# Decode attention on one core: masks from the identity, and cache rows dealt to the partitions in another order

## The chip, the cores and the metric

The kernel runs on one core of a Trainium2 chip. The metric is the device time of one execution in microseconds (us), as the median of several runs; lower is better. Beside it there is one profiled execution, whose trace gives every number below that has no other source.

## What is computed

Two decode-attention blocks, A and B, each for 4 batches, one query token, 32 query heads, 8 key/value heads and a head size of 128. Each projects `x` with `wq`, attends over its cache and projects with `wo`. A reads all 8192 cached tokens, B only the last 2048. Cut to what matters:

```
q = (x @ wq) in heads                         # 4 query heads share one kv head
s = einsum("bhqd,bhkd->bhqk", q, k) * 128**-0.5
o = einsum("bhqk,bhkd->bhqd", softmax(s), v)
out_A = o @ wo                                # k, v: all 8192 tokens
out_B = the same with k, v = the last 2048    # concatenated behind A
```

Softmax and the weighted sum run over all tokens of a head, so the order in which the tokens of one head are held does not matter, as long as keys and values are held alike and each stays with its head.

## The kernel before

**Units.** The work is cut into 20 units: first 4 of B (one batch each, all 8 kv heads), then 16 of A (one batch and one pair of kv heads each: `gp` is the pair). Every unit holds 4 MB of keys and 4 MB of values, as 128 partitions of 128 token slots of 128 bf16 numbers, in `K_sb` and `V_sb`, which have two slots each. For an A unit the source is one stretch of 128 rows of 32 KB (a row is 128 tokens); rows 0 to 63 belong to the first head of the pair, rows 64 to 127 to the second. Before the change partition p holds row p, so partitions 0 to 63 hold the first head. A B unit is loaded differently: K in two transfers of four heads, V in four of two heads, and there the source's outer dimension counts the row in the head and the next one the head, so that heads alternate along the partitions (L739).

**One unit.** TensorE transposes K through PSUM banks (`pe_T`, L271), ScalarE and VectorE copy the result to `KT_sb` (L299), and TensorE multiplies with the query (`pe_S`, L312). VectorE takes the maximum over the tokens of each partition (`dve_max`, L413), and `dve_addmask` (L430) adds `MASK[P]`, which is 0 where partition and column belong to the same head and -1e30 elsewhere; GpSimd then takes the maximum over the partitions (`pool_ar1`, L437), and `dve_submask` (L444) subtracts the mask again, so that the exponentials of a wrong head come out as zero. P @ V of the unit before follows (`pe_PV`, L327), and once for each head group the output projection.

**Order.** Each engine has a list of operations in `plan`, filled by `op`; `emit` and `emit_loop` write it out with its semaphore waits. TensorE, VectorE and ScalarE run in a loop of two units. All large loads are issued by SP's queue in the order in which `kv_load` (L722) is called: the two `wq` (into the V slots), K of unit 0, then for each u K of unit u and V of unit u-1, with a 1 MB piece of `wo` before some. A load waits for its slot to come free (the `w` lists in `kv_load`). The last unit's V comes in five pieces, and the last `wo` piece in eight.

**Setup.** GpSimd writes `MK` (`pool_mask0`, L522) and `MASK[0]` (`pool_mask1`, L530) by eight small memsets, then constants and zeros (`pool_setup0`, L537), then `ident` and `identf` (`pool_setup1`, L549) and `permE` (L557). It then issues two DMAs (L569 to L576) that copy the two halves of `MK` to the even and odd partitions of `MASK[1]`, in which heads alternate. `dve_msk` (L564) makes `MSK` and `SEL` from `ident`. TensorE waits for it before its loop (L594).

Of the kernel before, what the change touches and what calls it, by code (L numbers as in the profile page):

```python
# [7 lines left out]
F32 = mybir.dt.float32  # L8
I32 = mybir.dt.int32
ACTF = mybir.ActivationFunctionType  # L10
AX = mybir.AxisListType
# [3 lines left out]
def bass_concat_heads__gqa_block_cached__sliding_block_cached__decode_kernel(  # L15
# [16 lines left out]
    _, HKV, SK, DH = A_k_cache.shape  # L32
    HQ = A_wq.shape[1] // DH
    REP = HQ // HKV
# [3 lines left out]
    NT = SK // 64  # L38
    NSEG = 4
    TS = NT // NSEG  # L40
    C = 2 * REP
# [4 lines left out]
    BIG = 1.0e30  # L46
# [8 lines left out]
    NTH = NT // 2  # L55
# [4 lines left out]
    WQ = [A_wq, B_wq]  # L60
# [12 lines left out]
    with ExitStack() as es:  # L73
        block = es.enter_context(nc.Block())

        def sb(name, shape, dt):
            return es.enter_context(nc.sbuf_tensor(name, shape, dt))
# [4 lines left out]
        def sm(name):  # L82
# [7 lines left out]
        ident = sb("ident", [128, 128], BF16)  # L90
# [3 lines left out]
        RQ = [sb("RQ%d" % P, [128, Bn, NSEG, 2, 2 * C], BF16) for P in range(2)]  # L94
        RQc = sb("RQc", [128, 2, NSEG, 2, 2 * C], BF16)
        permE = sb("permE", [128, 2, 2, 64], BF16)
        MK = sb("MK", [128, NSEG * C], F32)
        MASK = [sb("MASKA", [128, C], F32), sb("MASKB", [128, NSEG * C], F32)]
        M1 = sb("M1", [128, NSEG * C], F32)
        M1m = sb("M1m", [128, NSEG * C], F32)  # L100
# [14 lines left out]
        ORx = sb("ORx", [C * Bn, C, C, 128 // C], BF16)  # L115
        MSK = sb("MSK", [C * Bn, C], BF16)
        SEL = sb("SEL", [C * Bn, Bn], BF16)
        OL = sb("OL", [128, C, Bn], BF16)
        oacc = sb("oacc", [Bn, D], F32)
        osb = sb("osb", [Bn, 2, D], BF16)  # L120
# [5 lines left out]

        names = ["k0", "k1", "kh", "v0", "v1", "vl0", "vl1", "vl2", "vl3", "vl4", "wl0", "wl1", "wl2", "wl3", "wl4", "wl5", "wl6", "wl7", "x0", "x1", "w0", "w1", "wo",
                 "out0", "out1", "out2", "Tq", "Td", "Ta", "S", "PV", "Ed", "Ea", "Eq", "vs", "sub", "exp", "otr", "otp",
                 "ocp", "Ef", "fin0", "fin1", "ar1", "SM", "msk", "pset", "setup", "pm0", "pm1", "oc", "ocB", "mk0", "mk", "mka", "perm", "rq"]
        sems = {n: sm("s_" + n) for n in names}  # L130

        K_sbf = K_sb.bitcast(F32)
# [26 lines left out]
                return sems["Ed"] if jobs[key[1]]["eng"] == "dve" else sems["Ea"]  # L159
            return sems["vs" if t in ("max", "maxc", "sum", "rcp", "os") else t]  # L160

        DMA_KEYS = ("K", "Kh", "KH", "V", "Vh", "VL", "WL", "x", "out", "WQ", "wo", "mk")

        plan = {e: [] for e in ("sp", "pe", "act", "dve", "pool")}
        turn = [None]
# [1 line left out]
        def op(eng, fn, waits=(), inc=None, bump=None):  # L167
            waits = list(waits)
            if not (eng == "pe" and turn[0] is not None):
                waits = [w for w in waits if w is not None]  # L170
            t = turn[0] if eng == "pe" or (eng in ("dve", "act") and turn[0] is not None and turn[0] >= T0P) else None
            plan[eng].append(dict(fn=fn, waits=waits, inc=inc, turn=t, bump=bump))
# [200 lines left out]
        def pe_job_OL(tn):  # L373
            idx = ol_idx[tn] = new_job("OL", "dve")
            bk = kbank(idx)

            def fn(pe):
                ins = None
                for r in range(C):
                    ins = pe.matmul(out=bk[:, r * Bn:(r + 1) * Bn], lhsT=ORx[:, r, :, :].rearrange("p o i -> p (o i)"),  # L380
                                    rhs=SEL[:, :], start=True, stop=True)
                return ins
            op("pe", fn, waits=[("E", ot_idx[tn]), bankfree(idx)], inc=("T", idx))

            def efn(dve):
                return dve.tensor_copy(out=OL[:, :, :].rearrange("p r b -> p (r b)"), in_=bk[:, 0:NR])
            return dict(eng="dve", fn=efn, waits=[("T", idx)], inc=("E", idx))
# [42 lines left out]
        def dve_addmask(u):  # L430
            n, P = ncol(u), units[u]["P"]

            def fn(dve):
                return dve.tensor_tensor(out=M1m[:, 0:n], in0=M1[:, 0:n] if P == 1 else M1c[:, :], in1=MASK[P][:, 0:n], op=AluOpType.add)  # L434
            return dict(eng="dve", fn=fn, waits=[("max", u, 1) if P == 1 else ("maxc", u)] + ([("mk", 1), ("mka",)] if u == 0 else []), inc=("pm", u, 0))

        def pool_ar1(u):  # L437
            n = ncol(u)
# [80 lines left out]
                w.append(("otr", 2 * tn - 2))  # L519
            return dict(eng="pool", fn=lambda pool: pool.tensor_copy(out=OTp[:, :, :], in_=OT_sb[:, P, q, :, :]), waits=w, inc=("otp", tn))  # L520

        def pool_mask0(pool):  # L522
            mkv = MK[:, :].rearrange("p (g s h) -> p g s h", g=NSEG, s=2)
            pool.memset(mkv[0:64, :, 0, :], 0.0)
            pool.memset(mkv[0:64, :, 1, :], -BIG)
            pool.memset(mkv[64:128, :, 0, :], -BIG)
            return pool.memset(mkv[64:128, :, 1, :], 0.0)
        op("pool", pool_mask0, inc=("mk0",))

        def pool_mask1(pool):  # L530
            pool.memset(MASK[0][0:64, 0:REP], 0.0)
            pool.memset(MASK[0][0:64, REP:C], -BIG)
            pool.memset(MASK[0][64:128, 0:REP], -BIG)
            return pool.memset(MASK[0][64:128, REP:C], 0.0)
        op("pool", pool_mask1, inc=("mka",))

        def pool_setup0(pool):  # L537
            pool.memset(dummy[:, :], 0.0)
            pool.memset(onesf[:, :], 1.0)
# [4 lines left out]
            pool.memset(oacc[:, :], 0.0)  # L544
            pool.memset(PT[:, :, :], 0.0)
            return pool.memset(Wo_sb[:, :, :], 0.0)
        op("pool", pool_setup0, waits=[("mk0",), ("mka",)], inc=("pset",))

        def pool_setup1(pool):  # L549
            ins = pool.affine_select(out=ident[:, :], in_=onesb[:, :], pattern=[[1, 128]],  # L550
# [12 lines left out]
        op("pool", pool_perm, waits=[("setup",)], inc=("perm",))  # L563
        def dve_msk(dve):  # L564
            idv = ident[0:NR, 0:NR].rearrange("p (h b) -> p h b", h=C)
            dve.tensor_reduce(out=MSK[:, :], in_=idv, axis=AX.X, op=AluOpType.max)
            return dve.tensor_reduce(out=SEL[:, :], in_=idv.rearrange("p h b -> p b h"), axis=AX.X, op=AluOpType.max)
        op("dve", dve_msk, waits=[("setup",)], inc=("msk",))
        for sh in range(2):  # L569
            m0 = MASK[1][:, :]  # L570
            pstm = m0.ap[0][0]
            dst_ap = bass.AP(tensor=m0.tensor, offset=m0.offset + sh * pstm, ap=[[2 * pstm, 64], [1, NSEG * C]])

            def mfn(pool, dst_ap=dst_ap, sh=sh):
                return pool.dma_start(out=dst_ap, in_=MK[64 * sh:64 * sh + 64, :])
            op("pool", mfn, waits=[("mk0",)], inc=("mk", sh))  # L576

        def dma(dst, src):
            def fn(e):
# [33 lines left out]
        assert pc == NC  # L613
        AFTER = {("S", 2): ("OT",), ("S", 5): ("OL",)}

# [106 lines left out]
        def kv_load(kind, u):  # L722
            un = units[u]
            cache = (KC if kind == "K" else VC)[un["P"]]
            buf = K_sb if kind == "K" else V_sb
            slot = u % 2
            if kind == "K" and slot == 1 and u < L:
                op("sp", lambda sp: sp.sem_inc(sems["kh"], 16), bump=(sems["kh"], 16, ("KH", u)))
            if un["P"] == 1:
                base = cache[un["b"], 0, SK - W:SK, :]  # L730
                hw = SK * DH
                n = NT // NPART[kind]
                for q in range(NPART[kind]):
                    if kind == "K":
                        w = [("T", tjob_idx[(u - 2, 8 * q + 7)])] if u >= 2 else []
                    else:
                        w = [("otr", u - 2)] if u >= 2 else [("T", tjob_idx[(1, 1)])] if u else [("T", qp_idx[(1, NQP - 1)])]
                    heads = HKV // NPART[kind]
                    src = bass.AP(tensor=base.tensor, offset=base.offset + q * heads * hw, ap=[[n * DH, W // n], [hw, heads], [1, n * DH]])  # L739
                    op("sp", dma(buf[:, slot, q * n:(q + 1) * n, :], src), waits=w, inc=(kind if q == NPART[kind] - 1 else kind + "h", u, q))  # L740
                return
            base = cache[un["b"], 2 * un["gp"], :, :]
            w = [("otr", u - 2)] if kind == "V" else [("otr", u - 3)] if u >= 2 * T0P else [("T", tjob_idx[(u - 2, NJ - 1)])]
            if kind == "V" and u == L:
                c0 = 0
                for i, n in enumerate(VCH):
                    t0, t1 = c0 * TC, (c0 + n) * TC
                    src = bass.AP(tensor=base.tensor, offset=base.offset + t0 * DH, ap=[[NT * DH, 128], [1, (t1 - t0) * DH]])
                    op("sp", dma(buf[:, slot, t0:t1, :].rearrange("p t d -> p (t d)"), src), waits=w, inc=("VL", i))
                    c0 += n  # L750
                return
            src = bass.AP(tensor=base.tensor, offset=base.offset, ap=[[NT * DH, 128], [1, NT * DH]])
            sem = sem_of((kind, u))
            bump = 16 * (NPART[kind] - 1)
            op("sp", lambda sp: sp.sem_inc(sem, bump), waits=w, bump=(sem, bump, None))
            if kind == "K" and u == L:
                for h in range(2):
                    t0 = h * NTH
                    src = bass.AP(tensor=base.tensor, offset=base.offset + t0 * DH, ap=[[NT * DH, 128], [1, NTH * DH]])
                    op("sp", dma(buf[:, slot, t0:t0 + NTH, :].rearrange("p t d -> p (t d)"), src), inc=(kind, u, 0) if h == 0 else ("KH", u))  # L760
                return
            op("sp", dma(buf[:, slot, :, :].rearrange("p t d -> p (t d)"), src), inc=(kind, u, 0))
# [4 lines left out]
        for u in range(1, NU + 1):  # L767
# [4 lines left out]
            if u % 2 == 0 and tn in pieces:  # L772
                P, q = pieces[tn]
                src = WO[P][q * C * DH:(q + 1) * C * DH, :].rearrange("(p r) n -> p (r n)", p=128)
# [4 lines left out]
        for i, n in enumerate(WCH):  # L779
            src = WO[0][(NSEG - 1) * C * DH:NSEG * C * DH, :].rearrange("(h p) n -> p h n", p=128)[:, h0:h0 + n, :]  # L780
# [140 lines left out]
        def _(pool):  # L921
            emit("pool", pool)


# [1 line left out]
_INS = ['A_x', 'A_k_cache', 'A_v_cache', 'A_wq', 'A_wo', 'B_x', 'B_k_cache', 'B_v_cache', 'B_wq', 'B_wo']  # L926
_OUTS = [((4, 1, 1024), 'bfloat16')]
# [23 lines left out]
```

## Time and profile before

| What | Value |
|---|---|
| median of 3 runs (lowest, highest) | 439.1 us (439.0, 439.85) |
| profiled execution, its own time | 439.48 us |
| span of the profiled execution | 437.7 us |
| time of that execution outside its span | 1.8 us |
| HBM read in the span | 184.56 MB |
| busy: PE, VectorE, ScalarE, GpSimd | 365.7, 209.5, 194.9, 29.0 us |

"Busy" is the time in which an engine has an instruction running. Matmuls overlap, so a busy PE is not one at its peak. The DMA rows of the page divide the span into 40 slices of 10.9 us: a digit is the mean busy share of the core's 16 DMA engines in tenths. Windows of the trace give busy time in each stretch with the number of instructions in parentheses, and at the end of a row the granted TensorE clock, the DMA share and the rate in GB/s. The DMA records of the trace list each packet that a DMA engine moved, with its start, its duration and its size, but not which of the 16 engines moved it.

### The profile page before, as it was taken

The page shows a single profiled execution, that of the slowest core. Times are in us where ns is not written, and L with a number is a line of the kernel's source. Part 1 is how long each engine was busy: PE and PEld are TensorE (multiplying, and loading weights), DVE is VectorE, ACT ScalarE, POOL GpSimd, SP SyncE. Part 2 cuts the span into 40 slices and gives each one's busy share as a digit, 9 for nine tenths or more (in the row PEclk, how much of TensorE's full clock was granted, in tenths as well). Part 3 has the DMA queues.
Part 4 walks back from the last instruction along what each step waited for, and adds up shares of the span by engine and source line. Part 5 has one row for each costly group of instructions (what it writes and reads, how often), then busy time and mean ns, then how long its engine had stood idle before and what let it go on. Part 6 is the DMA issues. An engine that isn't in the chain of part 4 may idle for free.

```text
span 437.7 us, 15534 instructions
## 1 busy us (share of the span) xinstructions
PE 365.7 (84%) x7174; PEld 338.4 (77%) x7184; DVE 209.5 (48%) x404; ACT 194.9 (45%) x249; POOL 29.0 (7%) x96
## 2 busy tenths in 40 slices
PE   0078998998998959895989598969888996989986
PEld 0068897997996949795979588868878786979975
DVE  0004555664564634563456347525653563455651
ACT  1024474473663625371735254424544462636530
POOL 7110000000000000000000000000100000000000
PEclk9999999999999988998999899969996998899999
DMA  8999999999999999999999999999999999999996
GB/s 339 425 424 416 430 414 431 416 442 410 444 431 431 421 442 431 431 431 431 431 431 431 431 431 427 436 429 431 416 446 431 431 432 431 431 431 422 440 407 245
DMA packets 11348, 184.75 MB, mean 422 GB/s; under 512 B 1300, under 2 KB 2376, under 8 KB 2632
## 3 DMA queue, kind: packets, MB, share of 16 engines
q1 hardware_dynamic: 11248, 184.56, 99.1%
q8 instruction: 8, 0.13, 0.1%
q14 instruction: 4, 0.03, 0.0%
q0 software_dynamic: 64, 0.02, 0.0%
q10 hardware_dynamic: 24, 0.01, 0.0%
HBM read 184.56 MB, written 0.01 MB: 422 GB/s over the span
## 4 chain that ended last, share of the span: by engine, by line
PE 51%; DMA 43%; issue 2%; DVE 1%; SPq 1%; PEld 1%; ACT 0%; PEldq 0%
DMA K_sb<-in_A_k_cache_dram 29%; PE KT L283 25%; PE OT L338 10%; DMA K_sb<-in_B_k_cache_dram 7%; DMA V_sb<-in_A_v_cache_dram 7%; PE SB L322 4%; PE SA L322 4%; PE KT L396 4%; PE SA L350 1%; SPq L580 1%; DVE oacc L404 1%; PE KT L338 1%; PEld OT L338 1%; ACT KT_sb L299 0%; PE KT L263 0%
## 5 line engine op out<-in xcount | busy, mean ns | idle before, releaser
L283 PE MATMUL KT<-identf,K_sb 128*128 128x128 f32 x1280 | 208.1, 296 | 42.9 <-DMA K_sb<-in_A_k_cache_dram 30.4
L299 ACT ACTIVATE KT_sb<-KT 128x1024 bf16<-128x1024 bf16 (+1 forms) x192 | 165.0, 881 | 119.8 <-PE KT L283 119.8
L283 PEld LDWEIGHTS KT<-identf,K_sb 128*128 128x128 f32 x1280 | 148.0, 150 | 48.1 <-DMA K_sb<-in_A_k_cache_dram 31.4
L299 DVE COPY KT_sb<-KT 128x512 int32<-128x512 int32 x160 | 110.4, 690 | 131.9 <-PE KT L283 130.5
L338 PE MATMUL OT<-PT,V_sb 128*128 128x64 bf16 x2560 | 78.1, 193 | 1.6 <-issue 0.9
L338 PEld LDWEIGHTS OT<-PT,V_sb 128*128 128x128 bf16 x2560 | 75.9, 98 | 1.8 <-issue 1.0
L469 ACT ACTIVATE PT<-Dt 128x512 bf16<-128x512 f32 x40 | 24.6, 630 | 84.0 <-DVE Dt L458 84.0
L322 PEld LDWEIGHTS SA<-RQc,KT_sb 128*128 128x128 bf16 x1280 | 57.0, 98 | 2.3
L322 PEld LDWEIGHTS SB<-RQc,KT_sb 128*128 128x128 bf16 x1280 | 51.0, 97 | 7.9 <-issue 4.4
L322 PE MATMUL SA<-RQc,KT_sb 128*128 128x16 bf16 x1280 | 56.4, 170 | 0.0
L322 PE MATMUL SB<-RQc,KT_sb 128*128 128x16 bf16 x1280 | 52.9, 170 | 0.0
L420 DVE TENSOR_REDUCE M<-SB 128x8 f32<-128x512 f32 (+1 forms) x20 | 13.8, 691 | 50.1 <-PE SB L322 50.1
L441 POOL PARTITION_ALL_REDUCE MB<-M1m x20 | 7.7, 385 | 333.7 <-DVE M1m L434 333.7
L396 PE MATMUL KT<-Wo_sb,OL 128*4 128x512 bf16 x80 | 18.9, 379 | 0.0
L201 PE MATMUL KT<-ident,x_sb 4*128 4x4 bf16 x8 | 0.5, 169 | 20.8 <-POOL identf L552 20.8
L201 PEld LDWEIGHTS KT<-ident,x_sb 4*128 4x128 bf16 x8 | 0.4, 111 | 21.0 <-issue 21.0
L476 DVE TENSOR_REDUCE LB<-SA 128x8 f32<-128x512 f32 (+1 forms) x20 | 13.7, 684 | 2.8 <-PE SA L350 2.8
L458 DVE TENSOR_TENSOR Dt<-SA,MBm 128x512 f32<-128x512 f32 x20 | 13.8, 691 | 0.7
L367 DVE TENSOR_TENSOR ORx<-KT,MSK 32x1024 bf16<-32x1024 bf16 x10 | 12.1, 1212 | 3.3 <-PE KT L362 3.3
L420 DVE TENSOR_REDUCE M<-SA 128x8 f32<-128x512 f32 (+1 forms) x20 | 13.6, 681 | 0.0
L458 DVE TENSOR_TENSOR Dt<-SB,MBm 128x512 f32<-128x512 f32 x20 | 13.6, 680 | 0.0
L350 PE MATMUL SA<-PT,onesb 128*128 128x128 bf16 x168 | 12.8, 218 | 0.0
(74 smaller groups left out, 119.5 us busy)
## 6 DMA issues: line engine op xcount, KB each, us to landing
K_sb<-in_A_k_cache_dram SPq DMA_DIRECT2D x15, 4096.0 KB, 22.5
V_sb<-in_A_v_cache_dram SPq DMA_DIRECT2D x15, 4096.0 KB, 30.6
K_sb<-in_B_k_cache_dram SPq DMA_DIRECT2D x8, 2048.0 KB, 23.9
V_sb<-in_B_v_cache_dram SPq DMA_DIRECT2D x16, 1024.0 KB, 18.7
V_sb<-in_B_wq_dram SPq DMA_DIRECT2D x1, 4096.0 KB, 12.4
V_sb<-in_A_wq_dram SPq DMA_DIRECT2D x1, 4096.0 KB, 22.4
Wo_sb<-in_B_wo_dram SPq DMA_DIRECT2D x4, 1024.0 KB, 12.0
K_sb<-in_A_k_cache_dram SPq DMA_DIRECT2D x2, 2048.0 KB, 17.9
```

The lines of the kernel that those rows point to most:

```text
L283: ins = pe.transpose(out=bkf[:, pi * 128:(pi + 1) * 128], in_=K_sbf[:, slot, t0:t0 + 2, :].rearrange("p t d -> p (t d)"), identity=identf[ ...
L299: ins = e.tensor_copy(out=d, in_=r) if eng == "dve" else e.activation(out=d, in_=r, func=ACTF.Copy)
L322: ins = pe.matmul(out=stb[:, t % NTH * C:(t % NTH + 2) * C], lhsT=ktv[:, pi, :, e], rhs=RQc[:, u % 2, t // TS, e, :], start=(e == 0), stop ...
L338: ins = pe.matmul(out=otb[:, s * NW:s * NW + w], lhsT=V_sb[:, slot, t, :], rhs=PT[:, slot, t * C:t * C + w], start=(j == 0), stop=(j == n ...
L350: ins = pe.matmul(out=SA[u % 2][:, s * NM:(s + 1) * NM], lhsT=onesb[:, :], rhs=PT[:, u % 2, c0:c0 + NM], start=(i == 0), stop=(i == n - 1))
L367: return dve.tensor_tensor(out=ORx[:, :, :, :], in0=bk[0:NR, 0:128].rearrange("p (i o r) -> p r o i", o=1, r=C).broadcast_to([NR, C, C, 12 ...
L396: ins = pe.matmul(out=bk[0:Bn, 0:D], lhsT=OL[:, i, :], rhs=Wo_sb[:, i, :], start=(i == 0), stop=(i == C - 1))
L420: return dve.tensor_reduce(out=M1[:, h * n:(h + 1) * n].rearrange("p (s h) -> p s h", h=C), in_=bank[:, :].rearrange("p (s j h) -> p s h j ...
L441: return pool.partition_all_reduce(MB[:, 0:n], M1m[:, 0:n], channels=128, reduce_op=ReduceOp.max)
L458: return dve.tensor_tensor(out=Dt[:, h * NTH * C:(h + 1) * NTH * C].rearrange("p (s j h) -> p s j h", s=Sh, h=C), in0=bank[:, :].rearrange ...
L469: return act.activation(out=PT[:, u % 2, a:b], in_=Dt[:, a:b], func=ACTF.Exp, scale=scale)
L476: return dve.tensor_reduce(out=LB[:, 0:n].rearrange("p (s h) -> p s h", h=C), in_=SA[u % 2][:, 0:NSEG * NM].rearrange("p (s j h) -> p s h ...
```

## The change

Two things. The masks are no longer written by memsets and DMAs: VectorE makes `EO[P]` from the identity, two numbers for each partition (1 in the column of the head that the partition holds, 0 in the other), and GpSimd makes `MASK[P]` as (EO - 1) * 1e30, repeated over the columns. The wait of the first `dve_addmask` follows.

And in A units every load of K and V deals the 128 source rows to the partitions in another order: partition 8j+m holds row 16m+j (j from 0 to 15, m from 0 to 7). Rows of 64 and more, the second head, are now those with m of 4 and more, so the heads alternate every four partitions, and `EO[0]` is made for that. Sizes, number and order of the loads, and all waits of the loads, are as before.

```diff
-            return dict(eng="dve", ..., waits=... + ([("mk", 1), ("mka",)] if u == 0 else []), inc=("pm", u, 0))
+            return dict(eng="dve", ..., waits=... + ([("mkb",)] if u == 0 else []), inc=("pm", u, 0))
...
-        def pool_mask0(pool):
-            mkv = MK[:, :].rearrange("p (g s h) -> p g s h", g=NSEG, s=2)
-            pool.memset(mkv[0:64, :, 0, :], 0.0)
-            pool.memset(mkv[0:64, :, 1, :], -BIG)
-            pool.memset(mkv[64:128, :, 0, :], -BIG)
-            return pool.memset(mkv[64:128, :, 1, :], 0.0)
-        op("pool", pool_mask0, inc=("mk0",))
-
-        def pool_mask1(pool):
-            pool.memset(MASK[0][0:64, 0:REP], 0.0)
...
-        op("pool", pool_mask1, inc=("mka",))
...
-        op("pool", pool_setup0, waits=[("mk0",), ("mka",)], inc=("pset",))
+        op("pool", pool_setup0, inc=("pset",))
...
         def dve_msk(dve):
             idv = ident[0:NR, 0:NR].rearrange("p (h b) -> p h b", h=C)
+            dve.tensor_reduce(out=EO[1][:, :], in_=ident[:, :].rearrange("p (i s) -> p s i", s=2), axis=AX.X, op=AluOpType.max)
+            dve.tensor_reduce(out=EO[0][:, :], in_=ident[:, :].rearrange("p (i s m) -> p s i m", s=2, m=4), axis=AX.XY, op=AluOpType.max)
             dve.tensor_reduce(out=MSK[:, :], in_=idv, axis=AX.X, op=AluOpType.max)
...
-        for sh in range(2):
...
-                return pool.dma_start(out=dst_ap, in_=MK[64 * sh:64 * sh + 64, :])
-            op("pool", mfn, waits=[("mk0",)], inc=("mk", sh))
+        def pool_mask2(pool):
+            for P, g in ((0, 1), (1, NSEG)):
+                ins = pool.tensor_scalar(out=MASK[P][:, :].rearrange("p (g s h) -> p g s h", g=g, s=2),
+                                         in0=EO[P][:, :].rearrange("p (g s h) -> p g s h", g=1, h=1).broadcast_to([128, g, 2, REP]),
+                                         scalar1=-1.0, scalar2=BIG, op0=AluOpType.add, op1=AluOpType.mult)
+            return ins
+        op("pool", pool_mask2, waits=[("msk",)], inc=("mkb",))
...
-                    src = bass.AP(..., ap=[[NT * DH, 128], [1, (t1 - t0) * DH]])
+                    src = bass.AP(..., ap=[[NT * DH, 16], [16 * NT * DH, 8], [1, (t1 - t0) * DH]])
...
-            src = bass.AP(tensor=base.tensor, offset=base.offset, ap=[[NT * DH, 128], [1, NT * DH]])
+            src = bass.AP(tensor=base.tensor, offset=base.offset, ap=[[NT * DH, 16], [16 * NT * DH, 8], [1, NT * DH]])
...
-                    src = bass.AP(..., ap=[[NT * DH, 128], [1, NTH * DH]])
+                    src = bass.AP(..., ap=[[NT * DH, 16], [16 * NT * DH, 8], [1, NTH * DH]])
```

More of the change, by code (lines that the diff above doesn't have):

```diff
@@ L96, in bass_concat_heads__gqa_block_cached__sliding_block_cached__decode_kernel @@
         permE = sb("permE", [128, 2, 2, 64], BF16)
-        MK = sb("MK", [128, NSEG * C], F32)
         MASK = [sb("MASKA", [128, C], F32), sb("MASKB", [128, NSEG * C], F32)]
@@ L117, in bass_concat_heads__gqa_block_cached__sliding_block_cached__decode_kernel @@
         SEL = sb("SEL", [C * Bn, Bn], BF16)
+        EO = [sb("EO%d" % P, [128, 2], F32) for P in range(2)]
         OL = sb("OL", [128, C, Bn], BF16)
@@ L128, in bass_concat_heads__gqa_block_cached__sliding_block_cached__decode_kernel @@
                  "out0", "out1", "out2", "Tq", "Td", "Ta", "S", "PV", "Ed", "Ea", "Eq", "vs", "sub", "exp", "otr", "otp",
-                 "ocp", "Ef", "fin0", "fin1", "ar1", "SM", "msk", "pset", "setup", "pm0", "pm1", "oc", "ocB", "mk0", "mk", "mka", "perm", "rq"]
+                 "ocp", "Ef", "fin0", "fin1", "ar1", "SM", "msk", "pset", "setup", "pm0", "pm1", "oc", "ocB", "mkb", "perm", "rq"]
         sems = {n: sm("s_" + n) for n in names}
@@ L160, in sem_of @@
             return sems["vs" if t in ("max", "maxc", "sum", "rcp", "os") else t]
-        DMA_KEYS = ("K", "Kh", "KH", "V", "Vh", "VL", "WL", "x", "out", "WQ", "wo", "mk")
+        DMA_KEYS = ("K", "Kh", "KH", "V", "Vh", "VL", "WL", "x", "out", "WQ", "wo")
         plan = {e: [] for e in ("sp", "pe", "act", "dve", "pool")}
@@ L434, in fn @@
                 return dve.tensor_tensor(out=M1m[:, 0:n], in0=M1[:, 0:n] if P == 1 else M1c[:, :], in1=MASK[P][:, 0:n], op=AluOpType.add)
-            return dict(eng="dve", fn=fn, waits=[("max", u, 1) if P == 1 else ("maxc", u)] + ([("mk", 1), ("mka",)] if u == 0 else []), inc=("pm", u, 0))
+            return dict(eng="dve", fn=fn, waits=[("max", u, 1) if P == 1 else ("maxc", u)] + ([("mkb",)] if u == 0 else []), inc=("pm", u, 0))
         def pool_ar1(u):
@@ L520, in pool_otp @@
             return dict(eng="pool", fn=lambda pool: pool.tensor_copy(out=OTp[:, :, :], in_=OT_sb[:, P, q, :, :]), waits=w, inc=("otp", tn))
-        def pool_mask0(pool):
-            mkv = MK[:, :].rearrange("p (g s h) -> p g s h", g=NSEG, s=2)
-            pool.memset(mkv[0:64, :, 0, :], 0.0)
-            pool.memset(mkv[0:64, :, 1, :], -BIG)
-            pool.memset(mkv[64:128, :, 0, :], -BIG)
-            return pool.memset(mkv[64:128, :, 1, :], 0.0)
-        op("pool", pool_mask0, inc=("mk0",))
-        def pool_mask1(pool):
-            pool.memset(MASK[0][0:64, 0:REP], 0.0)
-            pool.memset(MASK[0][0:64, REP:C], -BIG)
-            pool.memset(MASK[0][64:128, 0:REP], -BIG)
-            return pool.memset(MASK[0][64:128, REP:C], 0.0)
-        op("pool", pool_mask1, inc=("mka",))
         def pool_setup0(pool):
@@ L568, in bass_concat_heads__gqa_block_cached__sliding_block_cached__decode_kernel @@
         op("dve", dve_msk, waits=[("setup",)], inc=("msk",))
-        for sh in range(2):
[L570 to L575, printed above, removed]
-            op("pool", mfn, waits=[("mk0",)], inc=("mk", sh))
+        def pool_mask2(pool):
[5 more added lines that the diff above has]
+        op("pool", pool_mask2, waits=[("msk",)], inc=("mkb",))
         def dma(dst, src):
@@ L747, in kv_load @@
                     t0, t1 = c0 * TC, (c0 + n) * TC
-                    src = bass.AP(tensor=base.tensor, offset=base.offset + t0 * DH, ap=[[NT * DH, 128], [1, (t1 - t0) * DH]])
+                    src = bass.AP(tensor=base.tensor, offset=base.offset + t0 * DH, ap=[[NT * DH, 16], [16 * NT * DH, 8], [1, (t1 - t0) * DH]])
                     op("sp", dma(buf[:, slot, t0:t1, :].rearrange("p t d -> p (t d)"), src), waits=w, inc=("VL", i))
@@ L758, in kv_load @@
                     t0 = h * NTH
-                    src = bass.AP(tensor=base.tensor, offset=base.offset + t0 * DH, ap=[[NT * DH, 128], [1, NTH * DH]])
+                    src = bass.AP(tensor=base.tensor, offset=base.offset + t0 * DH, ap=[[NT * DH, 16], [16 * NT * DH, 8], [1, NTH * DH]])
                     op("sp", dma(buf[:, slot, t0:t0 + NTH, :].rearrange("p t d -> p (t d)"), src), inc=(kind, u, 0) if h == 0 else ("KH", u))
```

## The prediction

> **What bounds the kernel now.** I read the page's DMA rows first, since 184.56 MB in 437.7 us leave little room.
>
> ```profile
> DMA  8999999999999999999999999999999999999996
> GB/s 339 425 424 416 430 414 431 416 442 410 444 431 431 421 442 431 431 431 431 431 431 431 431 431 427 436 429 431 416 446 431 431 432 431 431 431 422 440 407 245
> ...
> q1 hardware_dynamic: 11248, 184.56, 99.1%
> ```
>
> Only the first and the last slices are not full: SP's queue q1 keeps 16 DMA engines busy 99.1% of the span. Windows then show whether anything else is full in the stages. The first row below is B units, the second and third are A units, the fourth is the end.
>
> ```profile
> 53.00:94.00 41.00, 39.05 (x765) 36.66 (x767) 23.19 (x42) 23.60 (x44) 1.53 (x5) 1.00 1.02 428
> ...
> 184.60:225.90 41.30, 35.28 (x677) 32.81 (x678) 21.07 (x41) 18.80 (x20) 1.81 (x8) 0.96 1.00 432
> 225.90:267.00 41.10, 34.98 (x676) 32.53 (x676) 21.07 (x41) 18.80 (x20) 1.78 (x7) 0.96 1.00 431
> 426.00:438.00 12.00, 7.79 (x165) 5.67 (x161) 2.43 (x7) 0.37 (x1) 0.20 (x1) 0.99 0.67 250
> ```
>
> The DMA share is 1.00 to 1.02 in both stages. In B, PE is near full as well (39.05 of 41.0 us); in A it has 6 us of slack in 41, and the waits of PE name who takes them:
>
> ```profile
> PE KT L283 <- DMA K_sb<-in_A_k_cache_dram: 30.4, 8, 5.2
> ```
>
> The chain of waits follows the compute in places, but only to the issue of a load that then stood in a queue:
>
> ```profile
> 184.65 21.00 DMA K_sb<-in_A_k_cache_dram
> 205.69 3.61 PE KT L283 x16
> ```
>
> That K takes 21.0 us from issue to landing; in the DMA records the loads land one after another, a 4 MB load every 9.71 us. I compared each issue on SP with the last landing of the load ahead of it: when a load is issued, at least 8.3 us of earlier work is still queued (issue at 123.87, the load ahead lands at 132.2). So the end is set by the sum of packet durations on 16 engines, not by when slots come free.
>
> Then the packets themselves, from the DMA records. From 100 us on there are 3726 packets of 32 KB: mean 1217 ns, standard deviation 7 ns, 98 in 100 between 1213 and 1225. Packets of 16 KB have a median of 614 to 615 ns, of 8 KB 312. The differences are in proportion to the bytes (1217 - 615 = 602 ns for 16 KB, 615 - 312 = 303 for 8 KB), with some 12 ns left over for each packet.[...]
>
> [...]
>
> **The change part by part.**
>
> *Masks, removed.* Eight memsets of about 0.1 us at 0.80 to 1.48 us on GpSimd: all of its setup moves forward by about 0.7 us. Two DMA issues on GpSimd, 1.39 us at 21.46, and their 64 packets: in the DMA records 512 bytes take 27 ns and a semaphore write 9, two of each on an engine, so 2 x 36 = 72 ns. DMA engines are the bound, so these 0.07 us come off the end.
>
> *Masks, added.* On VectorE two reductions of 128x128. Bounds: the 32x32 one took 174 ns, the 128x512 one 691; in proportion to the elements of a partition 174 + 96 x (691 - 174)/480 = 277 ns each, 0.56 us together. VectorE is idle from 21 to 35.28 us, and PE, which waits for `msk` before its loop, starts the loop at 34.05, when K of unit 0 has landed: 0 us on the path, with 12 us of cover. On GpSimd two small tensor_scalar operations; the nearest rows are the copies of 128x32 (0.21 us) and 128x128 (0.29 us), so 0.4 to 0.6 us in place of the 1.39. They wait for VectorE; queued behind them is the copy of RQc for unit 0, which ran at 26.55 and is first needed at 37.3 by the first L322. The mask is first read at 49.68; now it is ready at about 22.5. The lines that show this cover:
>
> ```profile
> 20.14 0.28 POOL L550 TENSOR_SCALAR_AFFINE_SELECT ident<-onesb 128x128 bf16<-128x128 bf16 x1 [11.22 <-issue]
> ...
> 21.46 1.39 POOL L575 DMA_DIRECT2D MASKB<-MK  x2
> ...
> 34.05 3.68 PE L283 MATMUL KT<-identf,K_sb 128*128 128x128 f32 x16 [2.60 <-DMA K_sb<-in_B_k_cache_dram]
> ...
> 49.68 0.19 DVE L434 TENSOR_TENSOR M1m<-M,MASKB 128x32 f32<-128x32 f32 x1
> ```
>
> The setup of 0.7 us earlier gains nothing: the first loop step waits for K. If the setup were late instead, the cover is 34.05 less the end of the RQ copy on ScalarE at 32.25: 1.8 us. In the loop the masks have the same shapes; nothing is added there.
>
> *Issue of the loads on SP.* A source with one dimension more: B's loads, which have that form, took 534 to 605 ns of SP for each issue, A's 328 to 375. With some 37 A loads at 0.2 us more each, each in its own place: SP has 8.3 us of cover at every issue, so 0 us. Behind SP's issue stand only later loads and the two small outputs. At the end, V's five pieces are issued 1 us later in sum; the eight `wo` pieces behind them took SP 16.57 us, far more than their issue needs[...].
>
> *The rows.* A's keys and values are 134.2 MB, that is 134.2e6/(16 x 32768) = 256 packets on each engine, 256 x 1.217 = 311.6 us. Every nanosecond on such a packet is 0.26 us. The row stays 32 KB long in the source and in the partition, so the packets stay 32 KB. Gain: if it were the order of the rows that costs the 12 ns left over, 256 x 12 = 3.1 us; but 8 KB, 16 KB and 32 KB packets all carry about the same remainder, whatever their pitch, so it belongs to the packet and I take 0. Loss: B's loads are the nearest rows. Their source, too, has a short outer dimension and an inner one that jumps by 2 MB from head to head. Their K packets of 16 KB have a median of 614 ns between 53 and 93 us, those of the last A unit's halved K, with plain rows, 615. Their V packets of 8 KB: 312, the plain `wo` pieces in A: 313. So neither the jump nor the dealing costs anything there, and I take 1217 ns again. The bounds to keep: -3.1 us, and the two rivals below.
>
> *Sum.* Against the profiled execution: 439.48 - 0.07 = 439.4, of which span 437.6. The median was 0.4 us below that execution, so I forecast 439.0 us.
>
> **Rivals.**
>
> [...]If half of the packets meet: 256 x 0.5 x 1.217 = 156 us more, 595 us; it shows as slower from 0.3% of packets that meet (0.003 x 311.6 = 0.9 us). Against it: B's loads would have met it, if they are split likewise, and did not.[...] 8%.
>
> *Row pitch (slower).* Neighbouring partitions now come from rows 512 KB apart.[...] Decides from 0.3% as above. Against it: B's K jumps by 2 MB at no cost[...]. In part[...] 8%, in full 6%.
>
> *Rows were a cost (faster).* What the 12 ns would give is 436.0 in full. Another source of gain is the drift between engines: the 16 completions of one load spread over 2.3 us by 105 us and 2.4 us at the end, and the slowest engine sets the end. It builds up in the loads of `wq` and in B, which the change leaves alone. 11%.
>
> *The rate of A is bound elsewhere and nothing is seen* is my forecast, 67%.
>
> **How the numbers follow.** The three runs differ by 0.85 us, so about 0.2% (0.9 us) is what can be told from no change. Same (438.2 to 439.9): 67%. Faster: 11%. Slower: 8 + 6 + 8 = 22%. The likeliest case gives 439.0. The range takes in that case, most of the faster one (to 437.0) and the partial loss (to 443): 67 + 7 + 8 = 82%; out are the full losses.
>
> **What would show it right or wrong.** Right: 32 KB packets at 1217 ns with the same small scatter, DMA share 1.00 in A, a 4 MB load every 9.7 us, q0 gone from the queues, MASKA and MASKB written by GpSimd near 22 us, A issues on SP near 0.5 us with no gap in the DMA rows. [...]Wrong by masks: L283 starting its loop later than 34 us. Faster: packets under 1213 ns, or completions of one load that spread over less than 2 us.

## The result, and the profile after

The changed kernel takes 775.3 us (770.2 to 777.9 in 4 runs) where the kernel before takes 439.2: a ratio of 1.763, 95% interval 1.756 to 1.770. The profiled execution took 770.19 us with a span of 768.1. The forecast of no change was wrong by more than 330 us.

The DMA rows of the page of the changed kernel, in slices of 19.2 us:

```profile
DMA  9999999999999999999999999999999999999996
GB/s 383 419 424 419 381 209 301 215 217 215 219 213 217 213 202 218 215 218 218 217 215 217 210 212 215 217 218 212 224 218 215 210 223 215 213 217 215 237 214 170
...
q1 hardware_dynamic: 11248, 184.56, 99.4%
```

The same bytes, the same number of packets, and all 16 engines as busy as before; but from the moment that A's loads begin (90 us on) they move half as much. Busy does not mean fast here: the share counts the time that packets take, so packets that take twice as long keep it at 99.4%. Windows of the same kernel, one of B units and one of two A units (busy times of PE, its weight loads, VectorE, ScalarE and GpSimd, in this order):

```profile
53.00:94.00 41.00, 38.85 (x762) 36.46 (x764) 23.05 (x41) 23.41 (x44) 1.54 (x5) 1.00 1.04 414
341.00:424.00 83.00, 41.21 (x675) 38.65 (x676) 21.08 (x41) 18.84 (x20) 1.96 (x8) 0.73 1.00 215
```

The turn of two A units, 41.2 us before, is 83. PE is now busy in half of it (matmuls overlap in these sums: eight of L322, 169 ns each by the median, are over 0.41 us after the first one's start), and its waits, before 30.4 us for A's keys, have become:

```profile
PE KT L283 <- DMA K_sb<-in_A_k_cache_dram: 235.9, 17, 18.8
PE OT L338 <- DMA V_sb<-in_A_v_cache_dram: 75.2, 15, 10.6
```

In the DMA records, the 32 KB packets of A have a mean of 2444 ns, and none between 150 and 700 us is below 1889; before it was 1217. B's packets are as before (16 KB: median 611 to 613 ns). The sum closes: 256 packets on each engine (of 32 KB, or as many bytes in smaller ones) x (2444 - 1217) = 314 us. The seven 1 MB pieces of `wo` have eight 8 KB packets on each engine; their mean rose from 313 to 595 ns, 56 x 0.282 = 16 us. Together 330 us, against 770.2 - 439.5 = 331 measured.

The masks went as forecast. Timeline of the changed kernel:

```profile
19.40 0.29 DVE L551 TENSOR_REDUCE EO<-ident 128x2 f32<-128x128 bf16 x1 [19.40 <-POOL identf L537]
19.60 0.28 DVE L552 TENSOR_REDUCE EO<-ident 128x2 f32<-128x128 bf16 x1
...
20.56 0.22 POOL L558 TENSOR_SCALAR MASKB<-EO 128x32 f32<-128x32 f32 x1
...
33.90 3.68 PE L283 MATMUL KT<-identf,K_sb 128*128 128x128 f32 x16 [3.76 <-DMA K_sb<-in_B_k_cache_dram]
```

The masks are ready at 20.8 us, and PE's loop still starts with the landing of K, at 33.90 (34.05 before). SP's issues of A loads take 0.54 us in place of 0.33 to 0.38, with no gap in the DMA row.

So the rows are what costs, and three theories remained, all of them assumptions at this point. *Write theory*: the form of the source decides which partitions the engines write at one time, and in this form engines disturb each other as they write; a packet of 2444 ns, twice 1217, suggests two at a time. *Row theory*: rows 512 KB apart, or 16 neighbouring rows at a time, collide in the memory. *Form theory*: a source with one dimension more is slow by itself.

### The profile page after: what moved, and what is told of

The parts are those of the page before. It is cut to its first block, busy times and chain, and to the rows that moved or that the text cites. A ratio compares the mean times of both kernels' runs of the same rounds, so it can differ in the third digit from the quotient of the medians.

```text
span 768.1 us, 15527 instructions
## 1 busy us (share of the span) xinstructions
PE 420.7 (55%) x7174; PEld 391.2 (51%) x7184; DVE 209.8 (27%) x406; ACT 195.4 (25%) x249; POOL 27.6 (4%) x88
## 3 DMA queue, kind: packets, MB, share of 16 engines
q1 hardware_dynamic: 11248, 184.56, 99.4%
## 4 chain that ended last, share of the span: by engine, by line
PE 47%; another core or an unknown queue 35%; DMA 17%; issue 1%; SPq 0%; ACT 0%; DVE 0%
PE KT L283 23%; PE OT L338 12%; DMA V_sb<-in_A_v_cache_dram 6%; DMA K_sb<-in_A_k_cache_dram 6%; DMA K_sb<-in_B_k_cache_dram 4%; PE SB L322 4%; PE SA L322 3%; PE KT L396 2%; PE SA L350 1%; PE KT L263 1%; SPq L566 0%; PE KT L380 0%; ACT KT_sb L299 0%; PE KT L700 0%
## 5 line engine op out<-in xcount | busy, mean ns | idle before, releaser
L283 PE MATMUL KT<-identf,K_sb 128*128 128x128 f32 x1280 | 227.6, 318 | 241.2 <-DMA K_sb<-in_A_k_cache_dram 235.9
L283 PEld LDWEIGHTS KT<-identf,K_sb 128*128 128x128 f32 x1280 | 166.0, 163 | 245.6 <-DMA K_sb<-in_A_k_cache_dram 237.9
L338 PE MATMUL OT<-PT,V_sb 128*128 128x64 bf16 x2560 | 108.2, 217 | 76.3 <-DMA V_sb<-in_A_v_cache_dram 75.2
L338 PEld LDWEIGHTS OT<-PT,V_sb 128*128 128x128 bf16 x2560 | 105.8, 115 | 77.8 <-DMA V_sb<-in_A_v_cache_dram 76.6
L322 PEld LDWEIGHTS SA<-RQc,KT_sb 128*128 128x128 bf16 x1280 | 58.8, 100 | 3.2
L322 PE MATMUL SA<-RQc,KT_sb 128*128 128x16 bf16 x1280 | 57.3, 171 | 0.0
L322 PEld LDWEIGHTS SB<-RQc,KT_sb 128*128 128x128 bf16 x1280 | 51.1, 97 | 7.9 <-issue 4.4
L322 PE MATMUL SB<-RQc,KT_sb 128*128 128x16 bf16 x1280 | 52.9, 170 | 0.0
L501 DVE TENSOR_REDUCE OS<-OT 128x8 f32<-128x32 f32 x15 | 2.9, 192 | 114.6 <-PE OT L338 114.6
L201 PE MATMUL KT<-ident,x_sb 4*128 4x4 bf16 x8 | 0.6, 170 | 19.5 <-POOL identf L537 19.5
```

What stands on the lines that cost most here:

```text
L283: ins = pe.transpose(out=bkf[:, pi * 128:(pi + 1) * 128], in_=K_sbf[:, slot, t0:t0 + 2, :].rearrange("p t d -> p (t d)"), identity=identf[ ...
L322: ins = pe.matmul(out=stb[:, t % NTH * C:(t % NTH + 2) * C], lhsT=ktv[:, pi, :, e], rhs=RQc[:, u % 2, t // TS, e, :], start=(e == 0), stop ...
L338: ins = pe.matmul(out=otb[:, s * NW:s * NW + w], lhsT=V_sb[:, slot, t, :], rhs=PT[:, slot, t * C:t * C + w], start=(j == 0), stop=(j == n ...
```

## Experiments

All are made from the changed kernel. "Plain rows" means partition p holds row p, with the source in one dimension of 128. Where no interval is given, a time is that of one execution, the profiled one; the kernel before took 439.1 to 439.4 us beside them. In the texts of what was expected, a forecast with no theory and no condition beside it is that of the write theory.

**The form alone, and a form with four partitions for each outer row.**

```diff
-  ap=[[NT * DH, 16], [16 * NT * DH, 8], ...]
+  ap=[[8 * NT * DH - DH, 16], [NT * DH, 8], ...]      # e1_form_plain_order, EO[0] for the two halves
+  ap=[[NT * DH, 32], [32 * NT * DH, 4], ...]          # e2_32x4, EO[0] with m=2
```

> The 16x8 form of the source with the rows in their old order: partition 8j+m holds row 8j+m, but each j starts one token (256 bytes) early, so that the two dimensions can't be merged into one of 128; a few tokens are therefore read twice and a few not at all, and the output differs from the reference. [...]packets of about 2450 ns, 770 to 778 us. Row theory (16 neighbouring rows, or rows 512 KB apart, collide in the memory): packets of 1217 ns, 439 us.

Measured: 761.1 us, A packets with a mean of 2414 ns. Windows of this kernel over A units:

```profile
150.00:550.00 400.00, 206.26 (x3362) 193.26 (x3365) 103.76 (x204) 93.08 (x99) 9.97 (x37) 0.72 1.00 218
```

Neighbouring partitions hold neighbouring rows again, as before the change, and yet the rate is 218 GB/s. The row theory falls; form and writes remain.

> Source dimensions 32 and 4: partition 4i+a holds row 32a+i[...]. [...]packets of 1217 ns and 439 us, equal to the kernel before within 0.2%. Row theory: slow[...]; 700 us or more.

Measured: 439.25 us, ratio 1.000 (0.9991 to 1.0008), packets of 1217 ns with a standard deviation of 10. Its window over two A units:

```profile
184.60:225.90 41.30, 35.66 (x681) 33.12 (x683) 21.07 (x41) 18.82 (x20) 2.01 (x8) 0.96 1.00 432
```

Again two source dimensions for the partitions, rows 1 MB apart in each four partitions, neighbouring rows in neighbouring fours, and nothing is lost: it isn't the second dimension and not the rows. Nothing is gained either, which answers what reading neighbouring rows brings.

**Eight outer rows.**

```diff
-  ap=[[NT * DH, 16], [16 * NT * DH, 8], ...]
+  ap=[[NT * DH, 8], [8 * NT * DH, 16], ...]           # EO[0] with m=8
```

> Source dimensions 8 and 16: partition 16j+m holds row 8m+j. [...]only 8 engines take part in an A load, each with 16 packets[...]: packets of about 2450 ns on 8 engines, a load every 39 us, 32 x 39 + 127 = 1375 us. If 8 engines take part and nothing clashes: packets of 1217 ns, a load every 19.5 us, about 750 us. Row theory: 16 engines as in the changed kernel, about 775 us.

Measured: 1135 us. From the page, the DMA rows (slices of 28.3 us) and the queue:

```profile
DMA  9999555465555554555645445455544545555542
GB/s 392 424 422 223 129 135 113 111 123 113 121 111 112 116 117 114 119 119 126 133 128 124 143 162 189 153 155 173 179 168 191 191 158 145 148 166 157 193 127 100
...
q1 hardware_dynamic: 10952, 184.56, 56.2%
```

The busy share in A halves (0.53 in the window from 150 to 250 us): 8 engines of 16, as many as the source has outer rows. The packets confirm it, 296 fewer than in the changed kernel (10952 against 11248), which is 8 completion writes fewer for each of the 37 A loads. From 150 to 450 us the packets have a mean of 2377 ns at 111 to 135 GB/s, a quarter of the full rate, as expected. Then the rate rises by itself, to 194 GB/s in the window from 850 to 900 us, where 81% of the packets are under 1300 ns on the same form of load. So the total was expected too high (1375), and the form theory is in trouble: one form, both speeds. What had changed meanwhile is how far the engines stand apart, as the completions show: those of one load spread over 4 us in the first A load, over 20 to 52 us in those that land after 520 us.

**The masks alone.**

```diff
-  ap=[[NT * DH, 16], [16 * NT * DH, 8], ...]
+  ap=[[NT * DH, 128], ...]                            # EO[0] for the two halves
```

> The masks from the identity, with the rows and the form of the source as before (EO for the first 64 and the last 64 partitions). All theories: 439.2 us, 0 to 0.2 us below the kernel before; if the masks had a part in the loss, it would be above 440.

Measured: 439.39 us, ratio 0.9999 (0.9991 to 1.0008). The masks cost nothing and gain nothing that can be told.

**The writes by themselves.** Ahead of the kernel with plain rows, five loads with nothing else moving:

```diff
+  for i, (k, m) in enumerate(((4, 8), (8, 8), (8, 4), (16, 4), (4, 16))):
+      src = bass.AP(..., ap=[[NT * DH, k], [k * NT * DH, m], [1, NT * DH]])
+      op("sp", dma(SC[0:k * m, :], src), waits=[("sc", i - 1)] if i else [], inc=("sc", i))
```

> The kernel with the new masks and plain rows, and ahead of all its loads five loads of 32 KB rows into an unused tile, one after another, each after the one before has landed, so that nothing else moves: source dimensions 4x8, 8x8, 8x4, 16x4, 4x16, in each partition m of outer row j being m + (inner size) x j from partition 0. [...]4x8[...]: 1217 ns. 8x8[...]: 2434. 8x4[...]: 1217. 16x4[...]: 2434. 4x16[...]: 2434. Row theory: no difference by where the partitions lie; 8x8 and 8x4 the same. If four or eight engines are slow whatever they write: 4x8 and 4x16 the same.

Measured, in the order of the loads, median of the packets: 1213, 2548, 1213, 2545 and 2468 ns. Windows inside the five loads:

```profile
4.00:12.00 8.00, 0.00 (x0) 0.00 (x0) 0.00 (x0) 0.00 (x0) 4.12 (x2) 1.00 0.27 115
17.00:34.00 17.00, 0.27 (x4) 0.21 (x4) 0.65 (x4) 0.39 (x2) 1.74 (x8) 1.00 0.50 104
39.00:42.00 3.00, 0.00 (x0) 0.00 (x0) 0.00 (x0) 0.00 (x0) 0.00 (x0) 1.00 0.61 262
47.00:54.00 7.00, 0.00 (x0) 0.00 (x0) 0.00 (x0) 0.00 (x0) 0.00 (x0) 1.00 1.00 206
62.00:92.00 30.00, 0.00 (x0) 0.00 (x0) 0.00 (x0) 0.00 (x0) 0.00 (x0) 1.00 0.24 55
```

Read the last two columns together. A packet counts in the window in which it starts, so the rate of a short window is rough: by their durations, eight engines with packets of 1213 ns move 216 GB/s, not 262. The busy shares of rows 1, 2, 4 and 5 (0.27, 0.50, 1.00 and 0.24 of 16 engines) agree with one engine for each outer row: 4, 8, 16 and 4. Rows 1 and 2: twice the engines move no more, 115 and 104 GB/s. Rows 2 and 3: as many outer rows, and both start with the same 32 rows, yet a packet takes 2548 and 1213 ns; only the partitions that are written differ. Rows 1 and 5 are such a pair too, 115 against 55 GB/s. Of the three theories only the write theory has this. All five came out within 5% of the forecast, but the estimate behind it, of which engines disturb each other, is not shown: the records name no engine.

**The dose.** The form of the first experiment for A's keys only:

```diff
+  form = [[8 * NT * DH - DH, 16], [NT * DH, 8]] if kind == "K" else [[NT * DH, 128]]
```

> Half of the dose: the 16x8 form in plain order (as in the form experiment, one token shifted for each j) for A's keys alone; A's values are loaded by plain rows of 128. Keys and values of some tokens no longer belong together, so the output differs from the reference. [...]128 packets on each engine at 2450 ns in place of 256: 439 + 128 x 1.23 = 597 us[...].

Measured: 679.9 us. Two windows, early and late:

```profile
150.00:320.00 170.00, 103.27 (x1841) 96.41 (x1842) 57.62 (x111) 53.20 (x56) 4.53 (x18) 0.78 1.01 280
400.00:600.00 200.00, 100.80 (x1610) 94.04 (x1613) 51.43 (x99) 47.06 (x50) 5.02 (x17) 0.71 0.91 240
```

Early a key load lands 19.5 to 19.9 us after the load ahead of it and a value load 9.4 to 11.7 us, near the forecast. Later the completions of one load spread over up to 39 us, and engines run out of work (share 0.91). The queue row of the page splits the 83 us above the forecast:

```profile
q1 hardware_dynamic: 11248, 184.56, 93.3%
```

The engines are idle for 6.7% of 678.0 us, 45 us, where it was 4 us before (0.9% of 437.7). So about 41 us are lost to idle engines, and the other half to packets longer than forecast; what made them longer is not shown.

**The phase.** If it is the moment that counts, engines that stand half a load apart may not disturb each other. A load with 12 outer rows of four gives 12 engines four packets more than the rest, by the count of engines above, and one with 4 gives four engines four more.

```diff
+  if u == Bn:                                   # ahead of the first A load; k=12, then k=4 (e7: k=12 alone, 8 in place of 4)
+      src = bass.AP(..., ap=[[NT * DH, k], [k * NT * DH, 4], [1, NT * DH]])
+      op("sp", dma(SC[p0:p0 + 4 * k, :], src), inc=("sc", i))
```

> The changed kernel with two loads into an unused tile ahead of the first A load[...]. [...]most A packets return to about 1217 ns, and the time to 450 to 480 us (439 plus 8 extra packets, 9.7 us, plus what clashes at the edges), as long as the offset isn't lost by engines that run out of work. If [...]the form itself makes a packet slow: 2450 ns and 780 us.

> The counterpart: one extra load with outer dimension 12, eight extra 32 KB packets[...]. [...]A packets stay near 2450 ns, 775 to 800 us. If any head start loosens the engines: as the head start of four.

> The head start of four in the kernel with the new masks and plain rows: what the extra loads cost by themselves. All theories: packets of 1217 ns and 439 plus up to 9.8 us (eight packets on the engines that have most), 445 to 450 us.

Measured: 623.3, 802.9 and 455.2 us. Windows over the A stage of the first two:

```profile
150.00:550.00 400.00, 260.79 (x4576) 243.62 (x4582) 140.64 (x275) 126.78 (x135) 12.85 (x48) 0.82 1.00 304
```

```profile
150.00:550.00 400.00, 194.98 (x3164) 182.57 (x3168) 96.82 (x192) 85.94 (x92) 9.81 (x36) 0.72 1.00 213
```

Against the changed kernel 152 us come back with four extra packets and nothing with eight (mean packet in that window 2468 ns), although both head starts put more packets on some engines than on others. But 304 GB/s is only part of the way (mean packet 1690 ns, 29% under 1300), the 450 to 480 us were missed, and the head start alone cost 16 us in place of up to 10. So the phase was tried with nothing else moving.

> The kernel with the new masks and plain rows, and ahead of all its loads three stages with nothing else moving, each after the one before has landed: four 4 MB loads in the 16x8 form of the changed kernel; the same after a head start of four 32 KB packets[...]; the same after a head start of four 16 KB packets, half as long. [...]packets near 2500 ns in the first stage; 1217 ns in the second but for its edges; in the third half of the packets at 1217 and half near 2500, mean about 1850 ns.[...]

Measured: 2508, 2090 and 2473 ns in the mean (32 KB packets; those of the second stage's head start are counted). The second and third are misses, though this head start was flawed: SP needed 1.6 us to issue it, so that the loads came 1.6 us behind and not at once; packets of up to 3.7 us, about three times 1213 ns, stand at the start of both stages. In the last run everything is queued behind two plain loads, and the head start fills the last four of each eight partitions.

```diff
+  loads = [two plain loads of 16 KB rows]
+  for k, tile in ((12, SC[:, :]), (4, SE[:, :])):
+      for i in range(4 if length else 0):
+          dst = bass.AP(..., offset=tile.offset + (4 + i) * prow, ap=[[8 * prow, k], [1, length]])
+  loads += [six loads with ap=[[NT * DH, 16], [16 * NT * DH, 8], [1, HR]]]
```

> A cleaner head start, since that of the two runs before was issued only 1.6 us ahead of the loads that it was to delay[...]. Kernel with the new masks and plain rows; ahead of all its loads three stages, each after the one before has landed. Each stage has two plain 2 MB loads, behind which everything is queued, then the head start, then six loads of 16 KB rows in the 16x8 form. Head start: none in the first stage; in the second four packets of 16 KB[...]; in the third the same with packets of 8 KB. [...]packets of 16 KB in the 16x8 form near 1275 ns in the first stage, 615 ns in the second, and in the third half of them slow, mean between 800 and 1100 ns.[...]

Windows in the three stages, behind the start of each:

```profile
14.00:68.00 54.00, 0.27 (x4) 0.21 (x4) 0.65 (x4) 0.39 (x2) 1.74 (x8) 1.00 1.01 214
91.00:115.00 24.00, 0.00 (x0) 0.00 (x0) 0.00 (x0) 0.00 (x0) 0.00 (x0) 1.00 1.02 401
136.00:190.00 54.00, 0.00 (x0) 0.00 (x0) 0.00 (x0) 0.00 (x0) 0.00 (x0) 1.00 1.01 226
```

With this head start the very form of the changed kernel runs at 401 GB/s (16 KB packets: mean 663 ns, 73% under 700) in place of 214 (1232 ns). Rows, form and engines are the same in both stages, so none of them is slow by itself; only the moment at which the engines write differs. Together with the five loads above, where only the partitions differed, the write theory is the one left that fits both: engines slow each other when they write at one time, in some partitions and not in others. The third stage was missed: half an offset should have relieved half of the packets. The mean fell by 5% to 1166 ns, and no packet in that window was under 1025 ns, so none was relieved. That the engines simply take turns is therefore not shown.

## Why the prediction was wrong

- *What bounds the kernel*: right. DMA was full, and the sum of packet durations set the end; for that reason a packet twice as long came through in full. (The cover at the issue at 123.87 us was 8.8 us by the landings, not 8.3; the least, 8.4 us, is at 309.19.)
- *Masks, issue on SP, setup*: right in that nothing of it reaches the end. The two reductions took 288 and 276 ns (277 forecast), the two masks 0.42 us, an A issue 0.54. GpSimd's setup came 1.3 us earlier (`ident` at 18.82 in place of 20.14 us), not 0.7. The 0.07 us at the end is too small for any run here to show.
- *The gain from neighbouring rows*: right at 0, by the 32x4 kernel.
- *"The rows. Loss"*: this step failed. I wrote "neither the jump nor the dealing costs anything there, and I take 1217 ns again", by B's loads. The packet took 2444 ns, and the term that I put at nothing was 314 us. B's loads show that a second dimension and jumps cost nothing; they don't show it for 16 outer rows of eight. B's outer rows fill two partitions (V) or four (K), the changed ones eight. The prediction has the objection itself, in "if they are split likewise", and the rival beside it got 8%: B's rate was evidence only under that condition, and it was assumed. One load of the changed form by itself would have decided it: in the first stage of the phase run, with nothing else moving, the packets of such loads took 2508 ns in the mean.
- *The rival in which packets meet (8%)*: right in its place, and in its packet (1217 + 1217 = 2434 ns by its sum, measured 2444). What it rested on, which engines meet, was the author's estimate and is not shown. Its size was wrong: I let half of the packets meet (595 us). In effect all were slow: between 150 and 700 us no packet was under 1889 ns, and 256 x 1.227 = 314 us. Why all and not half is not shown. The rival also left out the neighbours: the `wo` pieces lost 16 us, although their rows are plain. The completions of one A load lie 4 to 6 us apart, and a piece took 2.5 us before, so by my estimate they moved beside A's packets of other engines.
- *The rival "Row pitch"*: refuted at this size. Rows 1 MB apart in the 32x4 kernel cost nothing, and plain order in the 16x8 form cost nearly as much as the changed one (761.1 us). The 443 us for a loss in part were the author's estimate; no run here shows such a loss.

Left open: why half an offset gives so little; why the head start of four reached only 304 GB/s in the whole kernel; what made packets longer late in the keys-alone run; and which engines disturb each other, in which partitions. The records name no engine, and the rates show only which of the forms run here are slow. That holds for the 32x4 load too, with two outer rows for each engine: its packets of 1217 ns say that nothing was slowed there, not why.

## What to carry to other kernels

In these runs the source's dimensions decided how long a packet takes, and the order of the rows hardly: 16x8 had 2414 ns in plain order and 2444 in the changed one, 32x4 had 1217. Before a change of a source's outer dimension, time that very load with nothing else moving, and look at the length of its packets; the five loads above took 95 us together. If the rows of a load of 128 partitions must be dealt in another order, 32x4 is the form that cost nothing here (439.25 us), where 16x8 took 761.1 and 775.3 us and 8x16 1135. For a load of 64 partitions an inner dimension of four was not enough: 16x4 took 2545 ns for a packet. DMA engines that were 99.4% busy at half the GB/s, with packets at twice their length, were the sign here.

## What the runs showed of the hardware that was not expected

- In the slow forms a packet took a little longer than two of the fast ones (2 x 1213 = 2426 ns): with nothing else moving 2468 to 2548 ns for 32 KB, 12.9 to 13.3 GB/s for an engine in place of 27.0.
- The long packets did not ease in the changed kernel: no A packet between 150 and 700 us was under 1889 ns. With eight outer rows it did: at most 7% of the packets in any 50 us up to 650 us were under 1300 ns, then 35%, and the rate went from 114 to 194 GB/s.
- An offset of four of eight packets gave 401 GB/s, one of two packets 226, where none gave 214: there was no half-way relief.
- In the window in which PE waited more, the granted clock was lower: 0.96 in the window of two A units before, 0.73 in that after, with PE busy for half of the time in place of 85%. It is not simply the less, the lower: in the loads alone, where PE did nothing, the record has 1.00. It cost nothing that shows here, as PE waited 311 us for A's keys and values (235.9 + 75.2).
